# Loads, queues and row sizes of a planned block-sparse attention and MLP kernel

## The chip, the core and the metric

The kernel runs on one core of a Trainium2 chip. The core has a matrix engine (PE; its weight loads are listed apart as PEld), a vector engine (DVE), an activation engine (ACT), a general engine (POOL), and a queue engine (SP) that only issues transfers. SP and ACT issue transfers through hardware queues, POOL through a software queue; all of them end on the same 16 DMA engines. The metric is the device time of one execution in microseconds (us), the median of several runs. Before the change the median was 326.83 us over 3 runs (324.79 to 332.9).

## The reference

Four batches, eight heads, 768 positions of 64 values, in blocks of 32. A block of queries sees its own block and both neighbours, the first and the last block, and three sampled blocks; the first and last block of queries see everything. The output of attention, 3072 rows of 512, goes through a two-layer MLP with a gate.

```python
scores = scale * np.matmul(q, k.transpose(0, 1, 3, 2))
mask = np.abs(blk_i - blk_j) <= window
mask = mask | (blk_i == 0) | (blk_j == 0) | (blk_i == n_blocks - 1) | (blk_j == n_blocks - 1)
for qb in range(n_blocks):
    for kb in sampled_blocks[qb]:
        mask[qb * block:(qb + 1) * block, kb * block:(kb + 1) * block] = True
...                                   # softmax over the allowed keys -> attn
x = np.matmul(attn, v)                # (B, H, S, D) -> (B * S, H * D) = 3072 x 512
h = x @ w_in                          # 512 -> 2048
g = h * (1.0 / (1.0 + np.exp(-beta * h)))
out = g @ w_out                       # 2048 -> 512
```

Inputs and output are float32; the kernel computes in float16 with float32 sums.

## The kernel before

**Two kinds of attention work.** The 22 inner query blocks of a batch are taken two at a time: 11 pairs per batch, 44 in all, numbered n. For each pair and each of its two blocks (g), the eight key blocks that it sees (first, last, three sampled, three neighbours: 256 keys) are gathered from the transposed keys KT into a buffer KG by copies on POOL (L521) and on POOL or DVE (L259, tasks kn), and the eight value blocks are gathered into a buffer VG by transfers. Then come scores (PE L600 adds the mask, L610 multiplies), the maximum (DVE L621), the exponential (ACT L629), a reciprocal (DVE L635), the scaling of the probabilities (L641, POOL or DVE), eight transposes (PE L653), their copy to SBUF (DVE L657), and the product with VG (PE L668, 16 matmuls, "av"), whose result goes to xT by one copy on DVE or ACT each for two halves. The first and last block of each batch form "global" work with all 768 keys (L705 to L758).

**The V table.** Values are gathered by a number that is only known at run time, so the kernel first writes each batch's values as a float16 table VT of 768 rows x 512 to DRAM (1 KB a row), and the gathers read rows of it. For batch 0, V is loaded to a stage that lies in xT, cast to Vn in two halves (DVE L259) and written to VT in two transfers of SP (L490); later batches write it in one (L494). Per pair SP issues one transfer for the six neighbour blocks and six for the sampled blocks (L582, 32 rows of 1 KB each), two more on a batch's first pair for the first and last block; the buffers that come next in a batch copy these two blocks from the first one (tasks vres). Four VG buffers are used in turn: the gathers of pair n wait for av of pair n-4. Transfers of SP and ACT share eight completion lanes in turn, so that each waits for the one eight before it.

**Loads.** K, Q and V of batch 0 are loaded as float32 by SP (L388, half a tensor a transfer), K and Q into the buffers that later hold g. The weights are loaded by POOL and converted on the way: eight transfers of w_in (L417) and eight of w_out (L423), each written as 256 KB; a small copy (L403) holds them back until the first half of V has landed. K, Q and V of the later batches come the same way (L443, 18 transfers written as 384 KB each) into two float16 buffers RAW, and DVE reorders them half a tensor at a time (L259).

**The MLP.** Tokens are taken in groups of 8 or 16 blocks (256 or 512 columns): `sizes = [8, 8, 8, 16, 16, 16, 16, 8]`. A group's "h" is 16 steps of four matmuls with w_in (L817), then a tanh (ACT L823) and a product (DVE L828) into g; its "y" is 16 matmuls with w_out (L845) for each 128 tokens, an eviction (ACT L263) and a store (ACT's queue). xT holds the attention output of all four batches.

**The order of the work** is written out before the launch: a planner (class Plan) holds a duration, a priority, the engines allowed and the dependences of every task, simulates the engines, and emits the instructions of each engine in the order in which that simulation starts them. On the chip each engine keeps this order and waits where it must. Transfers are modelled as one shared pipe; `bulk` holds back a POOL load while that pipe is more than THR = 3.2 us behind. PSUM has eight banks, of which the MLP may hold four while attention is left.

```python
def emit_vg(n=n, f=f):
    o, i = f(held[n])
    nc.sync.dma_start(out=o, in_=i)
vg[n].append(add(f"vg{n}.{k_}", "SP", 0.5, emit_vg,
                 deps=[vv] + vtab[b] + ([av[n - NVG]] if n >= NVG else []),
                 prio=pr, dma=cost, hw=1))
```

## Time and profile before

| | |
|---|---|
| median of 3 runs | 326.83 us (324.79 to 332.9) |
| the profiled execution | 323.59 us, span of its instructions 321.8 us |
| PE busy | 280.7 us (87%) |
| DVE, ACT, POOL busy | 246.7, 216.8, 187.5 us |
| mean granted clock of PE | 0.929 |
| transfers | 43.97 MB, 137 GB/s on average |
| the chain that ended last | PE 60%, DMA 14%, DVE 12%, ACT 6%, issue 3%, SP's queue 3% |

The page divides the span by engine and line. A table by stage gives each engine's busy time in a stretch with the granted clock of PE and the share of the 16 DMA engines that was busy; the chain of waits follows the work that ended last back to what released each step. A busy PE is not PE at its peak: matmuls overlap, and at a granted clock of 0.50 the same work takes longer.

### The profile page before, as it was taken

To read this page: it belongs to the slowest core of one execution; us is meant where nothing else is said; L and a number is where in the kernel's file an instruction comes from. 1 tells how busy PE (TensorE), PEld (TensorE's weight loads), DVE (VectorE), ACT (ScalarE), POOL (GpSimd) and SP (SyncE) were. 2 spreads that over 40 slices of the span, in tenths; PEclk is the share of its full clock that TensorE was granted. 3 is DMA by queue.
4 is the path that set the end of the run, shared out by engine and by line. 5 is a ranking of instruction groups with operands and counts; after the bars stand their busy time and mean duration, and the time that the engine had idled before them with its cause. 6 is when DMAs were issued, how large, how long until landed. Compare 5 with 4: busy or idle time off the path is not lost.

```text
span 321.8 us, 10665 instructions
## 1 busy us (share of the span) xinstructions
PE 280.7 (87%) x3525; PEld 177.3 (55%) x3525; DVE 246.7 (77%) x572; ACT 216.8 (67%) x644; POOL 187.5 (58%) x528
## 2 busy tenths in 40 slices
PE   0845578989979699988979999999999999999994
PEld 0612366956755486556635656555665555554671
DVE  2996579878869989999987667999979975771060
ACT  1676435864968489789687669977679864772361
POOL 2479956848778456798966654756948453200000
PEclk9975557999979989999979999999999999999999
DMA  7889995998697586323777973335232333100201
GB/s 255 332 172 208 229 227 105 187 252 177 132 204 145 164 212 114 107 80 94 125 146 168 226 170 93 88 84 153 94 118 69 91 110 100 33 3 33 98 2 66
DMA packets 42211, 43.97 MB, mean 137 GB/s; under 512 B 6440, under 2 KB 37672, under 8 KB 42156
## 3 DMA queue, kind: packets, MB, share of 16 engines
q1 hardware_dynamic: 27760, 25.71, 27.1%
q0 software_dynamic: 10784, 11.27, 23.4%
q10 hardware_dynamic: 3612, 6.30, 5.4%
q8 instruction: 28, 0.46, 0.6%
q14 instruction: 27, 0.22, 0.2%
HBM read 45.10 MB, written 9.44 MB: 169 GB/s over the span
## 4 chain that ended last, share of the span: by engine, by line
PE 60%; DMA 14%; DVE 12%; ACT 6%; issue 3%; SPq 3%; POOL 1%; POOLq 0%; ACTq 0%; DVEq 0%
PE bank L845 22%; PE bank L817 21%; DMA VG<-VT 6%; PE bank L668 4%; PE bank L653 4%; DMA RAW<-in_k_dram 3%; DMA VT<-Vn 3%; SPq L582 3%; DVE ST L621 2%; ACT PP L629 2%; PE bank L463 2%; DVE g L828 2%; PE bank L610 2%; PE bank L600 2%; DMA sbl<-in_sampled_blocks_dram 1%
## 5 line engine op out<-in xcount | busy, mean ns | idle before, releaser
L641 POOL TENSOR_SCALAR PP<-PP,ST 128x256 f16<-128x256 f16 x168 | 81.3, 501 | 47.9 <-DVE ST L635 42.4
L629 ACT ACTIVATE PP<-bank,ST 128x256 f16<-128x256 f32 x176 | 81.6, 478 | 30.1 <-DVE ST L621 21.5
L817 PE MATMUL bank<-xT,w_in_sb 128*128 128x256 f16 (+1 forms) x512 | 97.1, 338 | 3.9 <-ACT PP L629 1.1
L845 PE MATMUL bank<-w_out_sb,g 128*128 128x512 f16 x384 | 90.9, 380 | 0.0
L828 DVE SCALAR_TENSOR_TENSOR g<-t,bank 128x512 f16<-128x512 f16 (+1 forms) x128 | 66.6, 546 | 22.1 <-ACT t L823 21.3
L823 ACT ACTIVATE t<-bank,beta_sb 128x512 f16<-128x512 f32 (+1 forms) x128 | 69.9, 589 | 14.3 <-PE bank L817 11.6
L817 PEld LDWEIGHTS <-w_in_sb 128*128 128x128 f16 x512 | 55.3, 116 | 30.1 <-issue 8.6
L521 POOL COPY KG<-KT 128x64 f32 x264 | 54.6, 256 | 24.6 <-PE bank L610 17.8
L621 DVE TENSOR_REDUCE ST<-bank 128x2 f32<-128x512 f32 x88 | 57.5, 678 | 7.5 <-PE bank L610 7.4
L845 PEld LDWEIGHTS <-g 128*128 128x128 f16 x384 | 34.7, 98 | 38.6 <-issue 4.1
L668 PE MATMUL bank<-PT,VG 128*128 128x64 f16 x704 | 31.8, 199 | 7.9 <-DMA VG<-VT 5.9
L668 PEld LDWEIGHTS <-VG 128*128 128x128 f16 x704 | 28.3, 102 | 16.5 <-issue 9.6
L629 ACT ACTIVATION_READ_ACCUMULATOR PP<-bank,ST 128x1 f32 x176 | 36.8, 209 | 0.0
L653 PE MATMUL bank<-identity,PP 128*128 128x128 f16 x352 | 30.9, 233 | 6.6 <-ACT xT L257 2.4
L653 PEld LDWEIGHTS <-PP 128*128 128x128 f16 x352 | 24.6, 104 | 15.9 <-issue 4.1
L657 DVE COPY PT<-bank 128x1024 f16<-128x1024 f16 x44 | 30.1, 684 | 4.1 <-PE bank L653 3.3
L259 DVE CAST xT<-bank 64x256 f16<-64x256 f32 (+1 forms) x52 | 20.6, 402 | 12.3 <-PE bank L668 7.5
L263 ACT ACTIVATE osb<-bank 128x512 f32<-128x512 f32 x24 | 14.4, 601 | 20.7 <-PE bank L845 20.7
L257 ACT CAST xT<-bank 64x256 f16<-64x256 f32 (+1 forms) x52 | 17.4, 346 | 15.4 <-DVE xT L259 6.3
L610 PE MATMUL bank<-KG,QT 64*32 64x256 f16 x704 | 20.9, 293 | 1.4 <-POOL KG L521 1.0
L726 ACT ACTIVATE PG<-bank,SG 128x384 f16<-128x384 f32 x32 | 18.4, 583 | 4.9 <-DVE SG L721 4.1
L600 PE MATMUL bank<-maskr,ones 64*32 64x192 f16 (+1 forms) x352 | 14.9, 272 | 5.7 <-ACT PP L629 5.5
(79 smaller groups left out, 256.6 us busy)
## 6 DMA issues: line engine op xcount, KB each, us to landing
VG<-VT SPq DMA_DIRECT2D x268, 32.0 KB, 2.6
VG<-VT SPq DMA_DIRECT2D x40, 192.0 KB, 2.9
out_dram<-osb ACTq DMA_DIRECT2D x20, 256.0 KB, 2.2
RAW<-in_v_dram POOLq DMA_DIRECT2D x6, 384.0 KB, 5.1
RAW<-in_k_dram POOLq DMA_DIRECT2D x6, 384.0 KB, 5.6
VT<-Vn SPq DMA_DIRECT2D x3, 768.0 KB, 6.1
RAW<-in_q_dram POOLq DMA_DIRECT2D x6, 384.0 KB, 6.5
w_in_sb<-in_moe_w_in_dram POOLq DMA_DIRECT2D x8, 256.0 KB, 5.9
```

Of the source, the lines that this page charges most:

```text
L521: nc.gpsimd.tensor_copy(out=kg32[:, g, :, (2 + r) * W:(3 + r) * W], in_=kt32[:, :, bass.ds(vals[3 * g + r], W)])
L610: nc.tensor.matmul(bk[u][hp * BLK:(hp + 1) * BLK, g * 256:(g + 1) * 256], lhsT=QT[b % 2][u * D:(u + 1) * D, hp, (i0 + g) * BLK:(i0 + g + 1 ...
L621: mx[n, u] = add(f"mx{n}.{u}", "DVE", 0.6, lambda n=n, u=u, sb_=sb_: nc.vector.tensor_reduce(out=sb_[:, 0, 2 * u:2 * u + 2], in_=bank(("S" ...
L629: nc.scalar.activation(out=pb[:, u, g, :], in_=bank(("S", n, u))[:, g * 256:(g + 1) * 256], func=AF.Exp, bias=sb_[:, 0, 2 * u + g:2 * u + ...
L641: (nc.vector if eng == "DVE" else nc.gpsimd).tensor_scalar(out=pb[:, u, g, :], in0=pb[:, u, g, :], scalar1=sb_[:, 2, 2 * u + g:2 * u + g + ...
L653: nc.tensor.transpose(out=o[:, s * P:(s + 1) * P], in_=pb[:, u, g, c * P:(c + 1) * P], identity=identity)
L657: ptv[n] = add(f"ptv{n}", "DVE", 0.61, lambda n=n: nc.vector.tensor_copy(out=PT[n % NPT], in_=bank16(("T", n))), deps=[tp[n]] + ([av[n - N ...
L668: nc.tensor.matmul(o[:, (g * NHP + hp) * 64:(g * NHP + hp + 1) * 64], lhsT=vgb[:, g, c, hp * P:(hp + 1) * P], rhs=pt[:, g, c, :, hp * BLK: ...
L817: nc.tensor.matmul(o[:, 0:TW], lhsT=w_in_v[:, c, f // 4, f % 4, :], rhs=xT[:, c, c0:c0 + TW], start=(c == 0), stop=(c == NHP - 1))
L823: lambda G=G, f=f, TW=TW, tt=tt: nc.scalar.activation(out=tt[:, 0:TW], in_=bank(("H", G, f))[:, 0:TW], func=AF.Tanh, bias=0.0, scale=beta_ ...
L828: lambda G=G, f=f, TW=TW, tt=tt, gg=gg: nc.vector.scalar_tensor_tensor(out=gg[:, f, 0:TW], in0=tt[:, 0:TW], scalar=1.0, in1=bank(("H", G, ...
L845: nc.tensor.matmul(o[:, :], lhsT=gg[:, f, s * P:(s + 1) * P], rhs=w_out_sb[:, f, :], start=(f == 0), stop=(f == N_FFC - 1))
```

## The change

**V table and gathers.** Batch 0's V casts rank ahead of the other casts of DVE, and the table goes out in one transfer. Two neighbouring rows of VT are taken as one row of 2 KB: a block of 32 keys fills 16 partitions of VG with two keys each, and a sampled block is one transfer of 16 rows. Key 2k sits in the first half of partition k, key 2k+1 in the second; the transposes of the probabilities (L653) therefore read every second column, and the matmuls L668 index VG by halves. There are five VG buffers instead of four. For the first four pairs the second block's sampled gathers are issued by ACT.

**Weights.** 16 transfers of w_in and 16 of w_out instead of 8 and 8, all but the first after the V table has landed; the small copy that held them back goes. The hidden units are numbered two to a row (NI = 2) instead of four. An h step waits only for its half of w_in, a y step for its quarter of w_out.

**Later batches.** K, Q, V (in this order) are loaded by SP, unconverted, half a tensor at a time into three float32 buffers RAW, and cast a quarter at a time by DVE; the casts of V may go to POOL.

**xT** holds two batches: batch b + 2 overwrites b, and its writes wait for the h steps that read the old columns.

**The planner** models three rings that take turns packet by packet, and the eight lanes; a transfer costs a number of packets and a time for each. The MLP may hold five banks. Groups are `[8, 8, 8, 8, 16, 16, 16, 8, 8]`, LAG is 4.5 instead of 3.5, and batch 0's global work waits for the scores of pairs 4 and 5. The scaling of the first four pairs is fixed to DVE. beta is brought in eight rows instead of four.

```diff
+class Rings:
+    START = {"SP": 0.4, "ACT": 0.4, "POOL": 1.5}
+    LAND = {"SP": 0.9, "ACT": 0.9, "POOL": 2.0}
...
-                    if t.bulk is not None and ring_at > now + t.bulk + 1e-9:
+                    if t.bulk is not None and rings.backlog("POOL") > t.bulk:
+                        continue
+                    if t.dma and e != "POOL" and lanes[issued % 8] is not None:
                         continue
...
-    NKG, NVG, NP, NPT, NT, NO, NG = 3, 4, 3, 2, 3, 3, 2
+    NKG, NVG, NP, NPT, NT, NO, NG, NR = 3, 5, 3, 2, 3, 3, 2, 3
...
-    RAW = [sb(f"RAW{i}", [P, H, J * D]) for i in range(2)]
+    RAW = [sb(f"RAW{i}", [P, H // 2, J * D], FP32) for i in range(NR)]
-    VG = [sb(f"VG{i}", [P, 2, 2, D_MODEL]) for i in range(NVG)]
+    VG = [sb(f"VG{i}", [P, 2, 2 * D_MODEL]) for i in range(NVG)]
-    xT = sb("xT", [P, NHP, N_TOK])
+    xT = sb("xT", [P, NHP, 2 * S])
-    plan = Plan(8, 4)
+    plan = Plan(8, 5)
...
-    tch = touch(w_in_sb[0:1, 0, 0:1], v_stage[0:1, 0, 0:1], v0ld[0], -58)
...
+    NI = 2
+    NACT, NDVE, GFIRST = 4, 4, 4
+    for f in range(2):
+        fs = slice(f * D_FF // 2, (f + 1) * D_FF // 2)
+        for c in range(NHP):
+            for ps in (slice(0, 64), slice(64, P)):
+                t_win.append(add(f"win{len(t_win)}.", "POOL", 0.55, lambda c=c, fs=fs, ps=ps: nc.gpsimd.dma_start(
+                    out=w_in_sb[ps, c, fs], in_=w_in_r[c, ps, fs]),
+                    prio=-50 + 0.1 * len(t_win), dma=(4, 0.174), bulk=THR))
+    for c in range(N_FFC // NI):
+        for ps in (slice(0, 64), slice(64, P)):
+            t_wout.append(add(f"wout{len(t_wout)}.", "POOL", 0.55, lambda c=c, ps=ps: nc.gpsimd.dma_start(
+                out=w_out_sb[ps, NI * c:NI * c + NI, :].rearrange("x i m -> x (i m)"), in_=w_out_r[ps, c, :]),
+                prio=-48 + 0.1 * len(t_wout), dma=(4, 0.174), bulk=THR))
...
+    ORDER = "KQV"
...
-                    tl = add(f"ld{nm}{b}.{f}", "POOL", 0.9, lambda t=t, raw=raw, b=b, f=f, hs=hs:
-                             nc.gpsimd.dma_start(out=raw[:, hs, :], in_=src6(t, b, f * HH, HH)),
+                    tl = add(f"ld{nm}{b}.{f}", "SP", 0.5, lambda t=t, raw=raw, b=b, f=f:
+                             nc.sync.dma_start(out=raw, in_=src6(t, b, HH * f, HH)),
+                             deps=stage_users[i - NR] if i >= NR else [],
+                             prio=(-40 if b == 1 else pr - 30) + 0.1 * (i % 6),
+                             dma=(32, 0.065), after=t_wout[-1:] if b == 1 else (), slack=SLACK)
...
+                        tc_ = add(f"cast{nm}{b}.{hp}", {"DVE": 0.55, "POOL": 1.6} if nm == "V" else {"DVE": 0.55}, None,
+                                  emit_cast, deps=[tl] + ([tr[b - 1, hp]] if tr else []), prio=pr - 5 * (nm == "V"))
...
-                    deps=[v0ld[f]], prio=-65))
-                vtab[0].append(add(f"vtab0.{f}", "SP", 0.45, lambda cs=cs, vt_rows=vt_rows: nc.sync.dma_start(
-                    out=vt_rows[:, :, cs], in_=Vn[0][:, :, cs]),
-                    deps=[vperm[0][f]], prio=-64, dma=1.3, hw=1))
+                    deps=[v0ld[f]], prio=-73))
+            vtab[0].append(add("vtab0", "SP", 0.45, lambda vt_rows=vt_rows: nc.sync.dma_start(
+                out=vt_rows, in_=Vn[0]), deps=vperm[0], prio=-64, dma=(8, 0.234)))
+            for t in t_win[1:] + t_wout:
+                t.deps += vtab[0]
...
-    x_of = lambda n: (n // NB * NB + (n - 1) % NB) * BLK
+    x_of = lambda n: (n // NB % 2 * NB + (n - 1) % NB) * BLK
...
-                for r, (c, s) in enumerate(((0, 2), (0, 3), (1, 0))):
-                    yield 0.1, lambda v, g=g, r=r, c=c, s=s: (
-                        vgb[s * BLK:(s + 1) * BLK, g, c, :], vt[bass.ds(v[3 * g + r], BLK), :])
+                for r in range(3):
+                    yield g, 1, lambda v, g=g, r=r: (
+                        vgb[(2 + r) * HB:(3 + r) * HB, g, :], two(vt[bass.ds(v[r], BLK), :]))
...
+            act = g == 1 and on_act
+                (nc.scalar if act else nc.sync).dma_start(out=o, in_=i)
...
-        nrm[n] = add(f"nrm{n}", {"POOL": 1.85, "DVE": 0.8}, None, emit_nrm, deps=[rc], prio=pr - 0.5)
+        nrm[n] = add(f"nrm{n}", {"DVE": 0.87} if n < NDVE else {"POOL": 2.2 if n < 8 else 1.85, "DVE": 0.85}, None, emit_nrm, deps=[rc], prio=pr - 0.5)
...
+            pk = pb[:, :, :, :].rearrange("x u g (k c) -> x u g c k", c=2)
-                                            in_=pb[:, u, g, c * P:(c + 1) * P], identity=identity)
+                                            in_=pk[:, u, g, c, :], identity=identity)
...
-                            lhsT=vgb[:, g, c, hp * P:(hp + 1) * P],
+                            lhsT=vgb[:, g, c * D_MODEL + hp * P:c * D_MODEL + (hp + 1) * P],
...
-                         [evQ[b, hp] for hp in range(NHP)], prio=pr, lat=0.2,
+                         [evQ[b, hp] for hp in range(NHP)] + ([sc[GFIRST + w // 2]] if b == 0 else []), prio=pr, lat=0.2,
...
+    t_win[0].deps.append(kg[1])
-    sizes = [8, 8, 8, 16, 16, 16, 16, 8]
-    ready = [3, 7, 10, 18, 25, 32, 40, 43, 49]
-    LAG = 3.5
+    sizes = [8, 8, 8, 8, 16, 16, 16, 8, 8]
+    ready = [3, 7, 10, 15, 21, 29, 36, 40, 43, 49]
+    LAG = 4.5
...
-            th = add(f"h{G}.{f}", "PE", 4 * (TW / 2400.0 + 0.003), emit_h, deps=xdeps + t_win,
+            th = add(f"h{G}.{f}", "PE", 4 * (TW / 2400.0 + 0.003), emit_h, deps=xdeps + t_win[f // 8 * 8:f // 8 * 8 + 8],
...
+        for m in range(m0, min(m0 + sz, NBLK - 2 * NB)):
+            for t in xw[m // NB * NB + 2 * NB + (m + 1) % NB]:
+                t.deps += [h for h in hs if h not in t.deps]
```

## The prediction

> **What bounds the kernel now.** First the table by stage, because the sum over the span mixes stages with different limits. The columns are the stretch, its length, the busy time (and number) of PE, PEld, DVE, ACT and POOL, the granted clock of PE, the DMA engines' busy share and GB/s.
>
> ```profile
> 0.00:26.00 26.00, 11.25 (x193) 7.41 (x194) 17.94 (x59) 13.52 (x37) 13.22 (x48) 0.88 0.86 251
> 26.00:54.00 28.00, 18.26 (x244) 12.46 (x241) 21.78 (x56) 13.77 (x53) 22.58 (x59) 0.56 0.88 193
> 54.00:96.00 42.00, 37.78 (x525) 28.95 (x532) 33.64 (x81) 30.43 (x92) 31.03 (x90) 0.92 0.94 190
> 96.00:160.00 64.00, 58.52 (x880) 39.63 (x879) 60.43 (x145) 50.49 (x161) 48.70 (x124) 0.97 0.55 130
> 160.00:281.00 121.00, 118.73 (x1500) 68.21 (x1498) 98.84 (x208) 91.29 (x270) 72.00 (x211) 0.99 0.46 117
> 281.00:322.00 41.00, 36.21 (x200) 20.62 (x198) 14.04 (x28) 17.34 (x34) 0.00 (x0) 0.98 0.11 40
> ```
>
> From 54 us on PE is busy 90 to 98% of each stage and its clock is nearly full: this part is bound by PE, with DVE close behind (94% from 96 to 160 us). Before 54 us PE has little to do, half of it at clock 0.56. So only the opening has time to give, and what it gives should reach the end, as all later work is queued behind it on PE. The chain of waits says what the opening waits for (start, length, what):
>
> ```profile
> 17.85 8.90 DMA VT<-Vn
> ...
> 30.33 6.78 DMA VG<-VT
> ...
> 37.49 7.29 DMA VG<-VT
> ...
> 51.80 1.60 DMA VG<-VT
> ...
> 53.83 3.32 PE bank L817 x16
> ```
>
> From 17.85 us to the first h at 53.83 us the chain is the V table, then the gathers of five pairs (80 matmuls of L668 lie in that stage) and SP's issues between them. Why they are slow stands in the transfers of 26 to 54 us (queue: packets, MB, share of 16 engines; issue: median us to landing), beside two rows of the stages from 90 to 160 and from 160 to 282 us:
>
> ```profile
> q0 software_dynamic: 1023, 3.24, 61.5%
> q1 hardware_dynamic: 2657, 2.11, 26.1%
> ...
> VG<-VT SPq DMA_DIRECT2D x31, 32.0 KB, 5.2
> ```
> ```profile
> VT<-Vn SPq DMA_DIRECT2D x1, 768.0 KB, 3.3
> ```
> ```profile
> VG<-VT SPq DMA_DIRECT2D x120, 32.0 KB, 2.2
> ```
>
> A small gather lands in 2.2 us when the engines are half idle and in 5.2 us beside the weights; the table took 8.9 us at the start and 3.3 us later. One packet of the weights' queue costs 28 x 0.615 x 16 / 1023 = 0.27 us of an engine, one of the gathers' 28 x 0.261 x 16 / 2657 = 0.044 us for 0.8 KB.
>
> **V table: -6.8 us.** Now the second V cast starts at 16.9 us behind six small KG copies, and the table lands at 26.75. With the casts first, the second follows the first (ends 15.7) and ends at 16.6; the transfer then has no weights beside it but one. 3.3 us is the same transfer's best row, 8.9 its worst; I take 3.3, since nearly nothing is left to share with: landing at 19.9.
>
> **Gathers: -9.7 us.** From 26.75 to 53.4 us the five pairs took 26.7 us. If the engines take the queues' packets in turn, a gather packet now waits behind a 0.27 us one: 0.8 KB per 0.31 us, times 16 engines, 40 GB/s; a pair of 384 KB would take 9.6 us if always crowded (it took 5.3 on average). The change doubles the gather's packet (2 KB: about 0.09 us) and halves the weights' (0.13 us, by halving the row): 2 KB per 0.22 us, 145 GB/s, 2.7 us a pair. SP's issue is as slow: seven at 0.32 to 0.42 us, 2.6 us, the first pairs relieved by ACT. I take 3.0 us a pair, and 2.0 us for the head blocks and the last landing: 17 us, last VG at 37. Bounds: 26.7 us (nothing gained) and 13 us (SP's issue alone).
>
> **The weights** start at 20 instead of 16.8 us. All 4.2 MB need 22 us of the engines at the row's 17.2 us for 3.24 MB; with 7.3 us for the gathers beside them they land by 49, as now (last issue 41.2 + 6.5). The first h needs only eight transfers of 128 KB, about 33 us: not late against x at 37. Their 32 issues on POOL at 0.53 us (L417, L423) are 8 us more; POOL loses 18 issues of L443 at 0.78 us, 14 us. POOL is at 81% in the opening and mostly waits for DVE behind it: 0.
>
> The rule here speaks against the change. The Trainium skill, "DMA: Bandwidth & Descriptors", section "Bandwidth", asks for transfers of at least 1 MiB, and its section on the anatomy of a DMA puts about 2.0 us fixed on each; as an estimate from that page, 16 more transfers are 32 us of the weights' stream if they don't overlap, and y would start that much later. This trace's weights, 5.9 to 6.5 us to landing but issued every 1.6 us, do overlap, so the sum stays at 0.
>
> **What is late next.** To pair 5, DVE did 39.7 us of work (17.9 + 21.8); from its first real work at 5.85 us it can't be done with all of it by 37. The change puts off batch 0's global work (four times about 2.2 us of DVE: L719, L721, L733, L734, L747), which is later caught up on a DVE that is 80% busy from 54 to 96 us. That costs something only where DVE is the bound, below.
>
> **DVE's own extra work.** 16 more MLP products of the small form: 16 x (2 x 0.413 - 0.680) = 2.3 us. Two more pairs scaled on DVE: 2.8 (four of 0.352 each). Casts: 24 of K and Q at 0.54 (L397, the same shape) are 13.0 against the 13.5 of all reorderings now; V's 12 are 6.5 if they stay on DVE, 0 if POOL has them. Copies of the head blocks: 16 instead of 12, on half the partitions with twice the elements, so up to 0.8 instead of 0.45 each: 0 to 9. I take 9 us of 5 to 19. Only from 96 to 160 us is DVE nearly full; that stage holds 64 of its 275 us: 9 x 64/275 = **+2 us** (1 to 19).
>
> **Strided transposes: +2 us.** No row has this stride (4 bytes). Contiguous probabilities (L653) take 0.45 us for eight on the chain at full clock; at a stride of 12 bytes (L745) six take 0.45 to 0.47, so 0.02 us more each, and 352 of them 6.6 us. The weight load at 8 bytes (L817) is 116 ns against 104 and 131, and 256-column h steps still run at full rate. Bounds 0 and 6.6; by the nearest row a third.
>
> **At nothing:** x in two batches (batch 2 writes x from about 155 us; the first three groups' h, 192 matmuls, are over by 130); K, Q, V of batch 1 behind the weights (six at 2.7 us, 49 to 65, while K now lands at 66.8 and 71.6); the sixth small group (PE's columns are the same); beta. If the cover of x goes, attention stops until the h is done, a few us.
>
> **Sum:** 323.6 - 6.8 - 9.7 + 2 + 2 = **311 us**, against the profiled execution's own time. That execution lies 3.2 us below the median of the runs shown; I keep 311. A measurement here tells about 2% from no change: 6.5 us.
>
> **Rival 1, SP's queue: slower.** The loads now share the gathers' queue and SP's program. In the opening six loads of this size behind each other land 2.7 us apart, so a batch's six hold the queue for 16 us. A pair lasts 5.5 us (22 in the stage from 160 to 281); five VG buffers allow 27 us ahead, less 5 for issue and landing: cover 22 us. So 16 us is hidden. But a load must also wait for its RAW buffer, and SP stands still with every gather behind it: at the 5.6 us that a later load takes to land now, six in turn are 33 us, 11 over, for three batches +33: 344 us. It decides above 3.7 us a load. For: SP is in order and RAW has three buffers for six loads. Against: the loads rank ahead of the gathers by three pairs and the casts are short.
>
> The Trainium skill ("DMA: Bandwidth & Descriptors", section "Queues, rings and completion order") says the same of the ring: one per issuing engine, consumed in ring order, in turn with the other queues. The first half is why a gather must wait; the second is what the sum of the gathers uses. The trace shows the gathers' 5.2 us, but no row here has both kinds in one queue.
>
> **Rival 2, the weights still crowd the gathers.** They are released by the same landing as the gathers. If the packet sizes don't matter, only the table's 6.8 us stays: 321 us, the first av at about 28 and the fifth at 47 us.
>
> **Rival 3, DVE becomes the bound.** If 19 us are added and the put-off work is not absorbed, 311 + 17 = 328 us: within 2%, with DVE at 95% from 60 us on. For: 94% already. Against: DVE is idle two thirds of the last 41 us.
>
> **Rival 4, it goes better.** Two stretches of PE's time after 54 us are lost to late partners (37.8 of 42, 58.5 of 64). With five MLP banks, five VG buffers and POOL free of 14 us of loads, half of these 9.7 us may go, and the two costs on top: 302 us.
>
> **How the numbers follow.** Forecast 311 (304 to 318): 0.48. Rival 1: 0.13, slower. Rival 2: 0.14, half of it just faster than 2%. Rival 3: 0.12, a sixth of it slower. Rival 4: 0.13. Faster by over 2%: 0.48 + 0.13 + 0.07 = 0.68; within 2%: 0.07 + 0.10 = 0.17; slower: 0.13 + 0.02 = 0.15. Leaving rival 1 out, the range runs from two us below rival 4 to two above rival 3: 300 to 330.
>
> **What would show it.** One write of the table landing near 20 us; the fifth av before 40 us and the first h right behind; the granted clock above 0.8 from 26 to 54; gathers beside weights landing in 3 us or less; the stages after the opening looking as now, with DVE a little fuller. Rival 1 shows as PE waiting at L668 for VG in the middle of a batch, and SP waiting for a cast. The prediction is wrong if such waits appear, or if the opening shrinks and the later stages grow by as much.

## The result, and the profile after

The change made the kernel slower: 348.61 us median (346.53 to 351.73, 4 runs) against 328.44 us for the kernel before on the same chip, a ratio of 1.068 with a 95% interval of 1.056 to 1.080. All ratios here compare only the undisturbed, fast runs of a kernel with those of the kernel before on the same chip, so they can differ from the ratio of two medians. The forecast was 311 us, in a range of 300 to 330. The profiled execution spans 344.8 us, 23.0 more than before.

The table by stage of the changed kernel, with the stretches of the prediction and one more at the end (the stretch, its length, busy time and number of PE, PEld, DVE, ACT and POOL, granted clock of PE, DMA share, GB/s):

```profile
0.00:26.00 26.00, 11.27 (x180) 7.51 (x180) 17.71 (x54) 11.92 (x30) 16.46 (x57) 0.80 0.70 236
26.00:54.00 28.00, 13.87 (x231) 10.14 (x231) 18.04 (x48) 12.26 (x51) 19.50 (x51) 0.63 0.89 179
54.00:96.00 42.00, 30.94 (x418) 22.30 (x416) 31.66 (x84) 28.41 (x84) 23.27 (x66) 0.94 0.78 226
96.00:160.00 64.00, 56.90 (x854) 40.15 (x853) 57.00 (x146) 50.07 (x162) 40.34 (x113) 0.96 0.57 170
160.00:281.00 121.00, 109.63 (x1420) 62.77 (x1417) 94.75 (x204) 87.10 (x270) 73.73 (x226) 0.96 0.44 131
281.00:322.00 41.00, 41.00 (x380) 23.83 (x379) 24.93 (x50) 26.04 (x65) 6.71 (x15) 1.00 0.21 65
322.00:345.00 23.00, 18.68 (x119) 11.36 (x116) 6.14 (x16) 8.68 (x20) 0.00 (x0) 0.97 0.13 46
```

PE is busy as long as before (282.3 us for 280.7), so the loss is PE's idle time. Take PE's column from that of before: it stands idle 4.4 us longer from 26 to 54 us (13.87 for 18.26), 6.8 from 54 to 96, 1.6 from 96 to 160 and 9.1 from 160 to 281, 22 us in all. DVE is no fuller in any of these stages than before: from 96 to 160 us it is busy 57.0 us for 60.4. So no engine has become the bound; something makes PE wait, and it does so in the opening and again far behind it.

The chain of waits of the changed kernel (start, length, what) shows both, first the opening, then what lies behind it:

```profile
17.93 4.86 DMA VT<-Vn
...
24.33 3.52 DMA VG<-VT
...
28.51 7.55 DMA VG<-VT
...
39.52 5.07 DMA VG<-VT
...
50.58 5.50 DMA VG<-VT
```
```profile
86.57 6.51 DMA RAW<-in_v_dram
93.10 1.03 DVE Vn L313 x2
...
128.42 4.83 DMA RAW<-in_v_dram
133.27 1.84 DVE Vn L313 x2
...
172.82 5.20 DMA out_dram<-osb
178.89 0.74 SPq L607
180.67 5.38 DMA RAW<-in_k_dram
186.55 0.56 DVE K L313
...
196.68 6.52 DMA RAW<-in_v_dram
```

In the opening the gathers still carry the chain. Far behind it the chain runs through four loads of the later batches, 23.2 us in all, each with a cast on DVE behind it. At 172.82 us stands a line that nobody expects there: a store of the output. SyncE had to wait for it, then issued a load of K, and DVE stood at that load's cast. The views of the waits (engine, line, what ended the wait: total us, times, longest) say who waits for stores. First the kernel before, SyncE, then PE:

```profile
SPq L582 <- DMA out_dram<-osb: 8.1, 4, 4.2
```
```profile
PE bank L668 <- DMA VG<-VT: 5.9, 8, 1.5
...
PE bank L817 <- DVE g L828: 1.1, 2, 0.7
```

and the changed kernel, SyncE, then PE:

```profile
SPq L653 <- DMA out_dram<-osb: 34.3, 12, 7.3
...
SPq L546 <- DVE Vn L313: 7.8, 1, 7.8
```
```profile
PE bank L739 <- DMA VG<-VT: 15.7, 7, 4.5
PE bank L890 <- DVE g L902: 8.8, 3, 4.6
...
PE bank L739 <- DVE ST L705: 6.0, 1, 6.0
```

L653 is the line that issues the gathers. SyncE was held there 34.3 us by stores, and the gathers and loads behind it were issued late. Gathers and stores have no data in common. What they share is the eight completion lanes: the trace shows one of eight semaphores on each of the 382 transfers that SyncE or ScalarE issues, given out in turn over both queues, and a transfer waits until the previous one on its lane has landed. (The Trainium skill, "DMA: Bandwidth & Descriptors", section "Why a DMA increments its semaphore by 16 and not by 1", gives a reason for such a wait: with two transfers in flight on one semaphore, its count doesn't say which of them has landed. No run here shows that; the wait itself is in the traces.)

How this reaches PE has to be read with care. Of PE's 15.7 us for gathers, 10.9 lie before 46 us, ahead of the first store (74.9 us). After 54 us its four longest waits are for DVE: 4.6 us at 91 us, 3.5 at 135, 6.0 at 189 and 2.4 at 199. Each comes right after DVE has stood at the cast of a load that hadn't landed (4.8, 2.8, 6.0 and 2.7 us). Two of these loads were issued soon after a store had held SyncE, until 84.4 and until 178.0 us; ahead of the other two SyncE was issuing gathers one after the other. So, as far as this trace shows, the stores of the changed kernel reach PE mainly by way of late loads and DVE, and they aren't the only reason why the loads are late.

### The profile page after: what moved, and what is told of

The parts are those of the page before. It is cut to its first block, busy times and chain, and to the rows that moved or that the text cites. A ratio compares the mean times of both kernels' runs of the same rounds, so it can differ in the third digit from the quotient of the medians.

```text
span 344.8 us, 10883 instructions
## 1 busy us (share of the span) xinstructions
PE 282.3 (82%) x3587; PEld 178.1 (52%) x3587; DVE 250.2 (73%) x596; ACT 224.5 (65%) x675; POOL 180.0 (52%) x524
## 4 chain that ended last, share of the span: by engine, by line
PE 45%; DMA 21%; DVE 17%; SPq 6%; issue 4%; ACT 3%; POOL 2%; ACTq 0%; POOLq 0%; DVEq 0%
PE bank L922 19%; PE bank L890 14%; DMA VG<-VT 9%; DMA RAW<-in_v_dram 5%; SPq L653 5%; PE bank L739 3%; PE bank L724 3%; DVE g L902 3%; DVE ST L691 2%; DMA out_dram<-osb 2%; DMA RAW<-in_k_dram 2%; DVE Vn L313 2%; DMA VT<-Vn 1%; DVE xT L313 1%; DMA g<-in_k_dram 1%
## 5 line engine op out<-in xcount | busy, mean ns | idle before, releaser
L711 POOL TENSOR_SCALAR PP<-PP,ST 128x256 f16<-128x256 f16 x152 | 71.9, 492 | 75.8 <-DVE ST L705 72.0
L897 ACT ACTIVATE t<-bank,beta_sb 128x256 f16<-128x256 f32 (+1 forms) x144 | 70.5, 553 | 19.4 <-DVE g L902 11.9
L902 DVE SCALAR_TENSOR_TENSOR g<-t,bank 128x256 f16<-128x256 f16 (+1 forms) x144 | 67.6, 501 | 15.6 <-ACT t L897 15.1
L739 PE MATMUL bank<-PT,VG 128*128 128x64 f16 x704 | 30.6, 199 | 24.3 <-DMA VG<-VT 15.7
L311 ACT CAST xT<-bank 64x256 f16<-64x256 f32 (+1 forms) x61 | 20.6, 348 | 32.0 <-PE bank L739 17.1
L724 PE MATMUL bank<-identity,PP 128*128 128x128 f16 x352 | 30.0, 231 | 3.0 <-ACT PP L699 1.5
L313 DVE CAST xT<-bank 64x256 f16<-64x256 f32 (+1 forms) x43 | 17.0, 402 | 21.1 <-ACT xT L311 13.2
L313 POOL COPY KG<-KT 128x384 f32<-128x384 f32 (+3 forms) x50 | 23.0, 483 | 0.0
L808 POOL TENSOR_SCALAR PG<-PG,SG 128x768 f16<-128x768 f16 x15 | 15.2, 1022 | 11.3 <-DVE SG L805 7.3
```

The source lines that it names most:

```text
L313: (nc.vector if eng == "DVE" else nc.gpsimd).tensor_copy(out=out, in_=in_)
L711: (nc.vector if eng == "DVE" else nc.gpsimd).tensor_scalar(out=pb[:, u, g, :], in0=pb[:, u, g, :], scalar1=sb_[:, 2, 2 * u + g:2 * u + g + ...
L724: nc.tensor.transpose(out=o[:, s * P:(s + 1) * P], in_=pk[:, u, g, c, :], identity=identity)
L739: nc.tensor.matmul(o[:, (g * NHP + hp) * 64:(g * NHP + hp + 1) * 64], lhsT=vgb[:, g, c * D_MODEL + hp * P:c * D_MODEL + (hp + 1) * P], rhs ...
L897: lambda G=G, f=f, TW=TW, tt=tt: nc.scalar.activation(out=tt[:, 0:TW], in_=bank(("H", G, f))[:, 0:TW], func=AF.Tanh, bias=0.0, scale=beta_ ...
L902: lambda G=G, f=f, TW=TW, tt=tt, gg=gg: nc.vector.scalar_tensor_tensor(out=gg[:, f, 0:TW], in0=tt[:, 0:TW], scalar=1.0, in1=bank(("H", G, ...
```

## Which part of the change costs it

**Parts taken back from the changed kernel.** Eight runs each undo or alter one part. The time of a run is given with its ratio to the kernel before; the changed kernel's is 1.068.

Loads of the later batches back on POOL, converting, as before:

```diff
-    RAW = [sb(f"RAW{i}", [P, H // 2, J * D], FP32) for i in range(NR)]
+    RAW = [sb(f"RAW{i}", [P, H // 2, J * D]) for i in range(NR)]
...
-                             nc.sync.dma_start(out=raw, in_=src6(t, b, HH * f, HH)),
+                             nc.gpsimd.dma_start(out=raw, in_=src6(t, b, HH * f, HH)),
```

> The loads of the later batches go back to POOL's queue and are converted on the way (float16 RAW, three buffers of half a tensor); all else stays as changed. Theory A, SP's order: the loads stand among SP's gathers, are issued late (their buffer, the eight lanes shared with the stores), and DVE, then PE, wait in order for the casts. Then DVE's waits for RAW (20.7 us over the span) fall below 8 us, the PE idle time of the stages 54 to 96 and 160 to 200 us (20.9 us together) falls below 10, and the time comes to 325 to 335 us. Theory B, the new plan as a whole (its ring model, group sizes, lag, x in two batches): PE keeps its idle time and the time stays at 342 to 352 us.

354.87 us, 1.094 [1.086, 1.102]: slower still, above the ranges of both theories. DVE no longer waits for a load of the later batches at all, as theory A had it, but PE now waits 28.7 us for gathers (15.7 in the changed kernel). So rival 1 of the prediction, that the loads on SyncE are what costs, finds no support, and DVE's waits for the loads don't explain the loss by themselves. What SyncE waits for in this run is, again, stores, and more than in the changed kernel:

```profile
SPq L653 <- DMA out_dram<-osb: 52.1, 10, 11.2
```

Stores of the output issued by POOL:

```diff
-                    nc.scalar.dma_start(out=out[base + row:base + row + P, :], in_=ob)
+                    nc.gpsimd.dma_start(out=out[base + row:base + row + P, :], in_=ob)
```

> The 24 stores of the result are issued by POOL instead of ACT, so that they hold none of the eight lanes that SP's gathers and loads use. Theory A1, lanes: SP waits 34.3 us for stores that ACT issues late, and what is behind (gathers, loads) comes late; without it SP's waits on stores are 0 and the time is 330 to 340 us. Theory B: SP has slack there, the time stays at 342 to 352 us, or rises as POOL waits for evictions.

342.04 us, 1.059 [1.052, 1.065], the edge of theory B's range. In this trace the stores that POOL issues carry other semaphores than those of SyncE and ScalarE, and L653 no longer waits for a store at all. DVE's waits for loads fell to 6.9 us, but PE still waited 17.1 us for gathers. By the ratios it is 0.9 points better than the changed kernel, which the intervals don't tell from nothing; and POOL's queue now carries 24 stores, so it isn't a clean price of the waits.

The loads assumed 4 us later by the planner, V loaded first, and the planner of before over the new transfers:

```diff
-    THR, SLACK = 3.2, 2.0
+    THR, SLACK = 3.2, 6.0
```

> The planner counts a later load as usable 6 us after it lands instead of 2, so the casts come later in DVE's order. Theory A2, DVE's order: DVE stands at casts whose load is late by a few us (20.7 us in all); with the casts put later these waits fall below 10 us and the time is 335 to 342 us. Theory A (the loads themselves come too late for the batch): the waits move to PE and POOL, the time is 343 to 355 us.

```diff
-    ORDER = "KQV"
+    ORDER = "VKQ"
```

> The loads of a later batch come in the order V, K, Q as before the change, instead of K, Q, V. If V being last makes the V table and the first gathers of a batch late (batch 1's table lands near 98 us, 30 us later than before the change), the first table of batch 1 lands before 85 us and the time falls by 4 to 10 us, to 338 to 344. If all six loads are late together, the time stays at 345 to 352 us, with the waits moved from V to K and Q.

```diff
-        rings = Rings()
-        lanes = [None] * 8
+        ring_at = 1.0
+        lanes = [0.0] * 8
```

> The changed kernel's transfers, tiles and groups, but ordered by the planner as it was: all transfers one shared pipe, a load counted as its packets times their time. Theory B1, the order: the ring model believes that gathers keep pace beside the weights (on the chip the fifth av starts 12 us later than planned, against 6 in the kernel before), and the order that it writes out makes engines wait; with the older planner the time falls to 325 to 338 us. Theory B2 or C (the MLP's share, or no single cause): 342 to 360 us.

355.26 us (1.096), 362.94 us (1.113) and 357.48 us (1.093): all slower than the changed kernel, the first two above both of their ranges. SyncE's waits on stores are 45.4, 59.9 and 38.4 us. A better due time or another order of the tasks wasn't what was missing.

xT for all four batches with the groups, lag and banks of before (and NVG = 4, NR = 2, to make room); and the opening without ACT's gathers, without the scaling fixed to DVE and without the wait of the global work:

```diff
-    xT = sb("xT", [P, NHP, 2 * S])
+    xT = sb("xT", [P, NHP, N_TOK])
-    plan = Plan(8, 5)
+    plan = Plan(8, 4)
-    sizes = [8, 8, 8, 8, 16, 16, 16, 8, 8]
+    sizes = [8, 8, 8, 16, 16, 16, 16, 8]
...
-    LAG = 4.5
+    LAG = 3.5
```

> The changed kernel with x kept for all four batches and the MLP's groups, lag and bank limit (four) as before; for the room, VG has four buffers as before and RAW two. Theory B2: two batches of x force a ninth group and with five banks the MLP crowds attention out of PSUM; undone, the time falls to 325 to 338 us. Otherwise 340 to 360 us.

```diff
-    NACT, NDVE, GFIRST = 4, 4, 4
+    NACT, NDVE, GFIRST = 0, 0, 4
...
-                         [evQ[b, hp] for hp in range(NHP)] + ([sc[GFIRST + w // 2]] if b == 0 else []), prio=pr, lat=0.2,
+                         [evQ[b, hp] for hp in range(NHP)] + [], prio=pr, lat=0.2,
```

> The changed kernel without the edits of the opening that lie outside the transfers: no gathers issued by ACT, no scaling fixed to DVE, batch 0's global work not held back. Theory B3: ACT stands 10.7 us behind its own gathers in the opening (its longest wait) and batch 0's global work comes late; undone, the time falls by 5 to 10 us, to 338 to 344. Otherwise 344 to 356 us.

355.53 us (1.086 [1.078, 1.094]) and 351.75 us (1.073 [1.064, 1.081]). Neither gives anything back.

The weights as before, 16 transfers released by the first half of V:

```diff
-            for t in t_win[1:] + t_wout:
-                t.deps += vtab[0]
+    tch = touch(w_in_sb[0:1, 0, 0:1], v_stage[0:1, 0, 0:1], v0ld[0], -58)
```

> The changed kernel with the weights as before: eight and eight transfers, released by the first half of V, an h step behind all of w_in. Theory W: 330 to 340 us. If the weights' place is not the cause: 345 to 358 us.

358.76 us, 1.111 [1.096, 1.126]. Nothing here either: in the changed kernel the new weights are worth 4 points.

**Parts added to the kernel before.** None of the eight made the kernel faster by more than the intervals allow. The 2 KB rows are not among the parts taken back: the changed kernel with 1 KB rows was not run. Instead the parts were added to the kernel before one by one. First the planner alone, all transfers as before:

```diff
-        ring_at = 1.0
-        lanes = [0.0] * 8
+        rings = Rings()
+        lanes = [None] * 8
```

> The kernel before, all its transfers, tiles and groups, ordered by the new planner, with packets and times of the old transfers stated in the new form. Theory B1: this alone makes it slower, 335 to 350 us. If the planner isn't the cause: 320 to 331 us, as before.

Then on top of it the 2 KB rows (with the gathers, head copies, transposes and av of the change), the weights (32 transfers behind a table of batch 0 in one), and both:

```diff
-    VG = [sb(f"VG{i}", [P, 2, 2, D_MODEL]) for i in range(NVG)]
+    VG = [sb(f"VG{i}", [P, 2, 2 * D_MODEL]) for i in range(NVG)]
```

> The kernel before under the new planner (which alone left the time where it was, 326.8 us) plus one part of the change: V gathered in rows of 2 KB with two keys a partition, and with it the strided transposes and the copies of the head blocks on half the partitions. If this part costs (rival: the strided weight loads of L653 and the head copies on half the partitions, up to 6.6 and 9 us by the prediction's bounds), 332 to 342 us; if it only halves the packets, 318 to 328 us.

```diff
-    tch = touch(w_in_sb[0:1, 0, 0:1], v_stage[0:1, 0, 0:1], v0ld[0], -58)
+            for t in t_win[1:] + t_wout:
+                t.deps += vtab[0]
```

> The kernel before under the new planner plus another part: the weights in 32 small transfers behind the V table, the table in one transfer. Theory W: weights that start after the table hold back the loads of batch 1, which come behind them, and crowd the gathers of pairs 0 to 4 instead of the table: 332 to 345 us, with the table near 23 us. Prediction's own step: the table and the gathers gain, 310 to 322 us.

> Both parts together on the kernel before. If the parts are independent, 327 plus the sum of what each alone adds. If the sum of gains in the prediction holds (table 6.8, gathers 9.7, costs 4), 311 to 318 us. What is then left to 348 us lies in the later loads, x in two batches, the groups and the opening's edits.

| on top of the kernel before | us | ratio [95%] | SyncE's waits on stores, us |
|---|---|---|---|
| the planner | 326.81 | 1.000 [0.996, 1.004] | 9.5 |
| and the weights | 325.36 | 1.007 [1.002, 1.012] | 0.4 |
| and the 2 KB rows | 342.23 | 1.057 [1.046, 1.069] | 46.6 |
| and both | 349.31 | 1.077 [1.064, 1.091] | 59.1 |
| the whole change | 348.61 | 1.068 [1.056, 1.080] | 34.3 |

**The 2 KB rows are the part that costs** on top of the kernel before: 5.7% alone. With the weights on top it is as slow as the whole change; the loads on SyncE, x for two batches, five VG buffers and the new opening together then make no difference that these intervals show. Each of them can still gain or lose something that another one hides. The weights alone fell between their two ranges (310 to 322 and 332 to 345), and both together lie far above the 311 to 318 of the prediction's gains.

**The rows or the order that the planner makes of them.** The planner sees other costs with the new rows and writes another order. So each kind of rows was run in the order of the other: the planner was told the costs of the old rows for the new ones, and the reverse.

```diff
-                             prio=pr, dma=(cost, 0.084)))
+                             prio=pr, dma=(max(1, round(cost / 0.05)), 0.05)))
...
-            vres = add(f"vres{n}", {"POOL": 1.9, "DVE": 0.7}, None, emit_vres,
+            vres = add(f"vres{n}", {"POOL": 0.9, "DVE": 0.5}, None, emit_vres,
```

> Gathers in rows of 2 KB as in the earlier run of that part alone (342 us), but planned with the costs of the old rows, so that every engine gets the same tasks in the same order as in the kernel before under the new planner (326.8 us); only the transfers' shapes, the head copies and the strided transposes differ. Theory R, the rows themselves cost (gathers into 16 partitions, head copies, strided weight loads): 338 to 346 us. Theory O, it is the order that the new costs lead to: 322 to 331 us.

```diff
-                             prio=pr, dma=(max(1, round(cost / 0.05)), 0.05)))
+                             prio=pr, dma=(cost, 0.084)))
...
-            vres = add(f"vres{n}", {"POOL": 0.9, "DVE": 0.5}, None, emit_vres,
+            vres = add(f"vres{n}", {"POOL": 1.9, "DVE": 0.7}, None, emit_vres,
```

> The opposite corner: the old rows of 1 KB, planned with the costs of the new ones, so that every engine has the tasks in the order of the slow kernel. Theory O: 336 to 348 us with SP standing 30 us or more for stores. Theory R: 322 to 331 us, SP's wait for stores below 15 us.

343.40 us, 1.046 [1.039, 1.052], and 324.65 us, 0.988 [0.981, 0.995]. The written order isn't it: the rows cost 4.6 points in the one and 7.0 in the other, 17 and 18 us by the medians. (The second of these kernels is 1.2% faster than the kernel before, the only one here that is.)

## What the rows do: the turn of the lanes

Two kernels now have the same tasks in the same order on every engine, and differ by 17 us: the planner with 1 KB rows, and the same with 2 KB rows. Their traces can be laid beside each other instruction by instruction. The lag isn't spread over the run. On DVE it grows from 1.3 to 4.2 us at 109 us, from about 5 to 11 at 146 to 147, and from 12 to 17 at 222 us (times of the kernel with 1 KB rows). Just ahead of the jump at 146 us, SyncE's waits from 130 to 160 us, first with 1 KB rows:

```profile
SPq L636 <- DMA out_dram<-osb: 2.9, 1, 2.9
```

and with 2 KB rows:

```profile
SPq L641 <- DMA out_dram<-osb: 9.4, 2, 8.9
```

After 132.0 us SyncE issued nothing until 142.2; the store that held it was issued by ScalarE at 139.5. The lane numbers in the two traces tell why. Laid out in turn, they show how many of SyncE's transfers stand ahead of each store. A transfer eight places behind a store must wait for it, so SyncE can be at most seven past a store that hasn't landed (unless that place belongs to another store: with 2 KB rows SyncE stood 14 past the seventeenth, held by the eighteenth):

| store | 1 KB rows: ahead in the turn / issued when the store was | 2 KB rows, same order | 2 KB rows, later turn (last experiment but one) |
|---|---|---|---|
| third | 112 / 116 | 109 / 115 | 111 / 117 |
| fifth | 149 / 155 | 138 / 145 | 149 / 155 |
| eighth | 208 / 209 | 200 / 206 | 212 / 218 |
| twelfth | 266 / 263 | 250 / 254 | 268 / 271 |

With 1 KB rows the twelfth store stands behind 266 of SyncE's transfers, with 2 KB rows behind 250. The lanes aren't given out by the planner but by the layer that records the program, presumably by an estimate of its own: nothing but the rows differs, but the layer itself wasn't examined. With the rows, stores come up to 19 places earlier (the eighteenth: 312 for 331), SyncE stands 4 to 7 places past most of them, and is held until the computation reaches the store. Here is what that does to PE in the kernel with 2 KB rows (chain of waits from 232 to 243 us):

```profile
232.79 2.18 DMA VG<-VT
...
235.11 0.78 POOLq L570
235.88 0.11 POOL VG L313
...
236.95 1.11 POOL KG L575 x6
238.06 0.89 POOL PG L796
...
238.99 0.84 PE bank L804 x6
```

A gather lands at 234.97; POOL, in order, has a head copy that waits for it (7.7 us in the view of POOL's waits), and behind that the scaling PG that PE needs. The late gather reaches PE by way of POOL's queue: PE stood 5.9 us, its longest wait after 54 us.

**Moving the stores in the turn.** Each store was made to depend on the last gather that stands ahead of it in the written order, which puts it later in the turn:

```diff
-                    nc.scalar.dma_start(out=out[base + row:base + row + P, :], in_=ob)
+                    behind(nc.scalar.dma_start(out=out[base + row:base + row + P, :], in_=ob))
...
+    def behind(store):
+        tc.add_manual_dep(store.ins, last_sp[0].ins.name, mybir.DependencyInfo(
+            mybir.DependencyClass.Sync, mybir.DependencyReason.DATA), reason="lane order")
```

> The 2 KB rows in the written order of the planner-only kernel, as before, but each store of the output now also depends on the last gather written ahead of it. Eight semaphores are dealt in turn to the transfers that ScalarE and SyncE issue, and the ninth transfer waits for the first; the dependence moves the stores later in that turn (the store that stood behind 250 gathers now stands behind 275; in the planner-only kernel it stands behind 266). Theory L, it is the turn: with 2 KB rows the stores stand 2 to 24 gathers earlier in it, SyncE is held by stores that the computation hasn't reached, and the gathers come late. Then SyncE's waits on stores fall from 47 us to under 10, PE's waits on gathers from 11.5 to about 5, and the time from 343 to 325-331. Theory R, the 2 KB rows cost by themselves (16 partitions a gather, head copies of 1.9 us on POOL and 0.67-0.79 us on DVE, strided transposes): 340-345, whatever SyncE waits for.

339.34 us, 1.037 [1.025, 1.050]: neither theory's number. SyncE's waits on stores fell as expected, to 0.8 us, and PE's on gathers to 3.2, but the new dependence is a wait of its own. ScalarE now stood at its stores until the gather had landed, and all that it does stood behind, 16.4 us in all. The two longest lines of its view of waits:

```profile
ACT PP L693 <- DMA VG<-VT: 6.1, 2, 4.2
ACT KT L317 <- DMA VG<-VT: 5.9, 1, 5.9
```

The trace has the same number of gathers issued as stand ahead of the store (75 of 75, 86 of 86, 118 of 118): the two queues had changed places. The same edit in the changed kernel:

> The changed kernel with the same dependence of each store on the last gather of SyncE written ahead of it, nothing else. The stores move from behind 62, 66, 103, 112, 147 ... 250 gathers and loads to 70, 77, 109, 122, 155 ... 266. Theory L: SyncE's waits on stores fall from 34.3 us to under 10 and the time from 348.6 to 328-336, more than the stores on POOL gained (342.0), since POOL's queue isn't loaded with them. Theory R: no better than 342, the time with the stores on POOL, where SyncE didn't wait for a store either.

352.16 us, 1.074 [1.060, 1.088], no better than the changed kernel. SyncE's waits on stores fell to 7.9 us as theory L had it, but PE's six longest waits after 54 us are now for ScalarE (17.9 us together), so this is no test of the turn either. So the dependence was put on the gather eight places earlier, which has landed by then:

```diff
-        tc.add_manual_dep(store.ins, last_sp[0].ins.name, mybir.DependencyInfo(
+        tc.add_manual_dep(store.ins, last_sp[-8].ins.name, mybir.DependencyInfo(
```

> As the run before with the 2 KB rows and the dependence, but each store depends on the gather eight places ahead of the last one written ahead of it, which has long landed when the computation reaches the store; so ScalarE isn't held at its stores as it was there (its stores stood exactly where the gathers were, and the time lost lay at the stores). The stores still stand later in the turn than without the dependence: behind 69, 79, 111, 114, 149, 169 ... 268 gathers for 69, 78, 109, 113, 138, 149 ... 250. Theory L: neither SyncE nor ScalarE is held by the other, SyncE's waits on stores stay under 12 us, ScalarE's on gathers under 5, and the time is 325-331. Theory R, the rows cost by themselves: 338-344, with the lag behind the planner-only kernel arising at gathers that land late or at head copies, and not at stores.

332.14 us, 1.016 [1.009, 1.022], against 1.046 [1.039, 1.052] without the later turn: 3.0 points of the 4.6, some 10 us, come back, and nothing of the rows has changed. It lies just above theory L's 325 to 331. ScalarE waits 3.8 us for gathers. SyncE still waits for stores, less than half as long as the 47.2 us before, but more than the 12 us that the theory allowed:

```profile
SPq L647 <- DMA out_dram<-osb: 20.2, 8, 5.8
```

The traces agree. The tasks of every engine are in the same order as before, and where DVE's lag behind the kernel with 1 KB rows had jumped to 11 and to 17 us it is now 5.6 and 6.5.

**About two thirds of what the rows cost in this kernel is the turn of the lanes** (3.0 points of 4.6; by the intervals, 2 to 4). The same dependence on the stores of the kernel with 1 KB rows, where SyncE waits 9.5 us for stores, was not run, so it isn't known how much of the gain that kernel would share. Of the last 1.6 points, 5 us, a part belongs to the rows themselves: 1.8 us of the lag (1.5 without the dependence) is there at 55 us, before the first store (77.9 us). How the rest divides between these waits and the rows stays open.

The same in the changed kernel:

> The changed kernel with each store dependent on the gather of SyncE eight places ahead of the last one written ahead of it. The stores move in the turn of the eight semaphores from behind 62, 66, 103, 112, 147, 154, 155, 187, 191, 250 gathers and loads to behind 63, 70, 103, 115, 148, 161, 162, 196, 204, 259. The same edit gave the 2 KB rows without the rest of the change 10 us back (a ratio of 1.0157 for 1.0457). Theory L, the turn is most of the loss here too: SyncE's waits on stores from 34.3 us to about 15, time 335-341. Theory D, in the changed kernel the transfers of the opening and of the loads on the gathers' queue cost more than the turn does: 342-348.

347.64 us (342.41 to 350.78), 1.059 [1.036, 1.082]: not to be told from the changed kernel's 1.068. In the profiled execution, 350.78 us, SyncE's waits on stores fell to 15.8 us, as theory L had it, but PE's for gathers did not fall (18.5 us for 15.7), and the median lies in theory D's range. The runs scatter too much to say more than that the later turn isn't worth 20 us there. In the changed kernel, then, the turn is shown to be at work (34.3 us of SyncE's waits, the store in the chain with a load, a cast and PE behind it), but what it is worth there stays open. It isn't all: from 26 to 54 us PE has 4.4 us less, before the first store. And where stores were given lanes of their own, the time was still 1.059.

## Why the prediction was wrong

**What bounds it** was read rightly for the opening, but "only the opening has time to give" was the first mistake: it left out that the later stages had time to lose. Their 90 to 98% held only while gathers and loads arrived ahead of need, and the 8.1 us that SyncE waited for stores stood in the profile of before. "What it gives should reach the end" isn't borne out either. The first h step began at 53.7 us before, at 57.3 in the planner-only kernel, at 48.4 with the weights on top and at 47.5 in the changed kernel. The first three are within 1% of each other, and the fourth is the slow one.

**The term that failed is one that isn't in the sum**: the lanes. The text ahead of the prediction says that the transfers of SyncE and ScalarE share eight lanes and wait for each other; the prediction moved, added and resized transfers on both queues, and priced each by its duration alone. The 2 KB rows were priced at two strided microseconds and up to 9 of DVE's for head copies. On the kernel before they cost 5.7%, 17 us in the unchanged order, and some 10 of these came back when the stores were moved later in the turn. None of the rivals named this. How much of the changed kernel's own loss is the turn isn't shown.

**V table, -6.8 us: it became -4.0.** It landed at 22.79 for 26.75. The transfer took 4.86 us, not the 3.3 of the row chosen; and the second cast began at 17.0, since the small KG copies still stood ahead of it, and it ended at 17.9 for an expected 16.6. SyncE's 7.8 us wait for Vn, above, ends there.

**Gathers, -9.7 us: nothing came.** The fifth av began at 52.7 us for 52.2 before, not at 37. A small gather beside the weights landed in 4.2 us for 5.2 before; 3 or less was expected. The transfers from 26 to 54 us of the changed kernel:

```profile
q0 software_dynamic: 1691, 2.78, 59.8%
q1 hardware_dynamic: 1378, 1.87, 24.0%
...
VG<-VT SPq DMA_DIRECT2D x6, 192.0 KB, 5.7
VG<-VT SPq DMA_DIRECT2D x28, 32.0 KB, 4.2
VG<-VT ACTq DMA_DIRECT2D x7, 32.0 KB, 5.0
```

The packets came out as forecast: 28 x 0.598 x 16 / 1691 = 0.16 us of an engine for one of the weights' (0.13 forecast), 0.08 for a gather's (0.09). But the hardware queues moved 1.87 MB in 28 us, 67 GB/s, not 145. Before, by the prediction's own rows, it was 2.11 MB, 75 GB/s, where the same working gave 40 when always crowded. So packets taken in turn aren't what sets the gathers' rate. What does isn't shown: eight lanes of 32 KB at 4.2 us a landing would give 62 GB/s, an estimate that leaves out the six gathers of 192 KB. The rate of 145 GB/s, and with it 3 us a pair, was the failing step; rival 2 was nearer, that packet sizes don't matter.

**Weights at nothing** holds as a price on the kernel before, 1.007 on top of the planner, but not in its steps: in the changed kernel the last weight landed at 64.9 us, not by 49.

**K, Q, V of batch 1 at nothing** failed in the changed kernel. Forecast were six loads from 49 to 65 us. The first was issued at 64.1 us, the last landed at 93.1, and batch 1's V table at 98.2 for 72.0 before; PE's wait of 4.6 us at 91 us stands right behind. What this cost the whole wasn't priced by a run: with the loads on POOL DVE's waits were gone and the time was longer.

**DVE's own work.** Busy time rose by 3.5 us (250.2 for 246.7), under the 9 forecast, and DVE is no fuller than before in any stage up to 281 us. Its parts by shape, changed kernel (partitions x elements, number, busy, mean ns, idle before):

```profile
L313 DVE COPY VG<-VG 32x2048 f16<-32x2048 f16 x16 | 11.8, 744 | 2.3 <-DMA VG<-VT 2.3
L313 DVE CAST Vn<-RAW 128x768 f16<-128x768 f32 x12 | 8.0, 709 | 10.2 <-DMA RAW<-in_v_dram 10.2
L313 DVE CAST K<-RAW 128x768 f16<-128x768 f32 x12 | 7.0, 618 | 6.0 <-DMA RAW<-in_k_dram 6.0
L313 DVE CAST Q<-RAW 128x768 f16<-128x768 f32 x12 | 6.4, 570 | 4.5 <-DMA RAW<-in_q_dram 4.5
```

Casts of 21.4 us for 19.5 forecast, head copies of 0.74 us for up to 0.8: the sizes were close. The idle time ahead of the casts, 20.7 us, wasn't foreseen: DVE, in order, stands at a cast until the load has landed, and PE's four longest waits after 54 us stand behind such times. It isn't DVE's work that the prediction missed, but its waiting.

**Strided transposes, +2 us: nothing.** Before and after:

```profile
L653 PE MATMUL bank<-identity,PP 128*128 128x128 f16 x352 | 30.9, 233 | 6.6 <-ACT xT L257 2.4 <-DVE PP L641 2.0 <-POOL PP L641 1.5
```
```profile
L724 PE MATMUL bank<-identity,PP 128*128 128x128 f16 x352 | 30.0, 231 | 3.0 <-ACT PP L699 1.5 <-DVE PP L711 1.3
```

**x for two batches at nothing** holds, as far as the run with all four tells.

**Rival 1** came close in time (344 us), and that is luck: its price was six loads in turn at 5.6 us, each waiting for its RAW buffer, and the loads' own line waited 1.9 us for everything together. (The six loads of the opening, its other row, landed 2.0 us apart and not 2.7.) Gathers waited 6.5 us for loads on their lanes. SP waiting for a cast, one of its signs, hardly showed (0.3 us at that line), and giving the loads back to POOL made it slower. "SP, in order, is held, and every gather behind it" was right; what held it most were stores. The Trainium skill ("DMA: Bandwidth & Descriptors", section "Queues, rings and completion order") speaks of a ring in order per issuing engine, and by that alone a store on ScalarE's ring shouldn't hold a gather on SyncE's; the 34.3 us show that here the completion semaphores tie the two rings together.

## What to carry to other kernels

Before a transfer is moved, added or resized, look at which semaphore it shares with what: where a queue that runs ahead (gathers) and one that runs with the computation (stores) take their lanes in one turn, the first is held a few transfers past the second (with eight lanes, seven, where the eighth is its own), and the view of the issuing engine's waits shows it as a wait for a transfer that it has no business with. The order written for each engine isn't the whole order; where two builds keep it and differ in time, lay their traces beside each other and look at where the lag jumps. And when taking parts back explains nothing, add them to the old kernel one by one, and look which part was never taken back: four runs found here a part that the eight before had left in place.

## What the runs showed of the hardware that wasn't expected

- Half the packets bought the gathers nothing: with the 2 KB rows in the planner-only kernel's order the hardware queues carry 19056 packets for 27760, and a 32 KB gather lands in 2.5 us (median) for 2.6.
- A copy of the same bytes on half the partitions took 1.6 to 1.8 times as long: head copies of 64 x 1024 took 0.45 us on DVE before, of 32 x 2048 0.74 in the changed kernel; on POOL 1.03 us (planner alone) became 1.88.
- A transpose that reads every second column of float16 takes as long as one that reads them all (231 and 233 ns).
